# Nystrom attention and two feed-forward layers: scores of both factors in one group of 64x32 products, and k and q of batches 2 and 3 turned by VectorE

## The chip, the core and the metric

One NeuronCore of a Trainium2 chip. The metric is the device time of one execution in microseconds (us); of several runs the median is compared.

## The reference, cut to what matters

Four batches, eight heads, 576 rows, head size 64. Attention is approximated with 32 landmarks per head, the means of 18 rows each, and its output feeds two feed-forward layers.

```
q_lm = q.reshape(B, H, 32, 18, D).mean(axis=3);  k_lm likewise
A  = softmax(q    @ k_lm.T / 8)      # 576 x 32
Bm = softmax(q_lm @ k_lm.T / 8)      # 32 x 32
C  = softmax(q_lm @ k.T    / 8)      # 32 x 576
Z  = six steps of 2 Z - Z @ Bm @ Z   # from a scaled Bm.T
x  = A @ Z @ C @ v                   # to 2304 x 512
h  = x @ w_in;   x = (h * cos(h)) @ w_out          # 512 -> 2048 -> 512
h  = x @ w_in2;  y = prelu(h, alpha) @ w_out2
```

The weights arrive as 64-bit floats and are made into 32-bit ones on the chip.

## The kernel before, in words

**Units.** Attention is computed in eight units, one per batch and group of four heads: `u0`, `u1` (batch 0) and `U2` to `U7` (batches 1 to 3). A unit loads k, q and v, turns k and q so that the head dimension lies on partitions (`kt`, `qt`: two heads hh in the two halves of the partitions, two values bb in the free dimension), forms the landmarks `kq`, and computes two score tables: "c" (k against q's landmarks, tile `sc`) and "a" (q against k's landmarks, tile `sa`). The c table becomes exponentials, is turned and multiplied with v; the a table is turned in 32x32 blocks by VectorE (line 831), made a softmax, turned again and split into two parts for the matmuls of the ticks.

**How batches 2 and 3 turn k and q (`U4` to `U7`).** The load (line 635) is two DMAs of 288 KB for each of k and q, in runs of 256 bytes. TensorE then turns them with 18 transposes of 128x128 per unit (lines 684 and 693), and ScalarE or VectorE copies them out of PSUM: four copies of 512 columns and two of 128. `U2` and `U3` do the same; `u0` and `u1` have their own form. For `U4` to `U7` GpSimd sums the landmarks from `kt` and `qt` (line 727).

**How the scores are formed (`scores`, line 751).** `kq` is kept as block-diagonal pairs of heads: GpSimd sets it to zero once (line 510), and only the halves that belong to a head are written. A product has all 128 partitions as contraction, 64 landmark columns (two heads of 32) and 320 or 256 columns of the sequence. Each table of a unit is four products, two bb times two chunks; the two bb write to different halves of the output's partitions. In `U2` to `U7` the c table is one group of four products and the a table another, each into a pair of "x" banks of PSUM.

**Ticks.** The first feed-forward layer is 128 ticks (`t0` to `t127`). Each has six products h1 (line 1028) into one of two "h" banks, five elementwise steps on ScalarE and VectorE (lines 1033 to 1040; the split of line 397 on GpSimd or VectorE), and four times three products y1 (line 1053) into four "acc" banks. The "h" bank comes free with the product of line 1038 on VectorE. V' (`v_mm`, line 984) prepares each batch's attention for the ticks: eight products of 64 rows by 32 columns by 512, whose row half is bb and whose column group qd is worked out in the loop. After the ticks the second layer runs by a Strassen scheme (lines 1342 to 1423).

**Order.** The string `ORDER` lists every operation as unit:number, with a letter where the engine isn't the first choice (/V VectorE, /A ScalarE, /G GpSimd). Each engine, and SP's queue of DMAs, issues what falls to it in that order and waits in place. `w` operations are fill products on TensorE (line 520).

Of the kernel before, what the change touches and what calls it, by code (L numbers as in the profile page):

```python
# [11 lines left out]
I32 = mybir.dt.int32  # L12
# [8 lines left out]
u0:1 u0:2 u0:4 w:2 w:9 u0:11 w:7 w:6 w:8 w:10 u0:18 u0:7 u0:5 u0:9 u1:1 c2:1 u0:19 u1:2 u0:10/V u0:20 u0:6 u0:21 u0:12  # L21
u0:16 u0:17/V u0:8 u0:24 u0:22 c3:1 u1:4 u1:18 u0:14 u0:13/V c2:2 u0:23 u0:25 u0:26 u0:28 c2:3 c2:4 u0:15/V c3:2 u1:19
u1:20/A u1:21/A w:3 w:1 c3:3 z0:1 u0:27 z0:2 c1:1 z0:3 u0:3 c3:4 u1:5 z0:4 u1:6 w:5 u1:7 u1:8 z0:5 c1:2 z0:6 c1:3 z0:7
z0:8 z0:9 z0:10 z0:11 c1:4 z0:12 u0:31 u1:9 u1:10 u0:29 w:4 u1:22 u1:24 u1:11 u0:37 c0:1 c9:1 u1:23 u1:25 u0:34 z0:13
z0:14 u1:26 u0:30 c0:2 z0:15 u1:16 u1:17 u1:27 u1:28 u0:32 z0:17 z0:16 u1:12 w:11 c0:3 u1:31 u1:14 z0:18 u0:35 u1:13
u1:32 u1:29 c0:4 u1:30 u0:38 u1:34 c9:2 u0:33 u0:39 u1:3 u1:35 c9:3 u1:33 U2:1 u0:36 u1:36 u0:40 z0:19 u1:15 c9:4 u1:37
z0:20 u0:41 w:12 U2:4 u1:38 z0:21 z0:22 u1:39 u1:40 z0:23 z0:24 w:13 c10:1 c11:1 U2:2 u0:42 u0:43 z0:25 w:15 z0:26 w:14
c11:2 u0:44 u0:45 c10:2 w:16 z0:27 z0:28 u1:41 U2:5 U2:6 u1:42 u1:43 z0:29 u1:44 u1:45 c10:3 c4:1 U3:2 U2:13 z0:30 u0:46
U2:14 u0:47 z0:31 c10:4 U2:16/A U2:15/A z0:32 u1:46 z0:33/A z0:34 u0:48 v0:1 v0:2 u1:47 c11:3 v0:3 v0:4 u1:48 v0:5 w:17
U2:10 U2:12/V c4:2 u1:49/V u0:49 U2:11 U2:17 U2:18 U2:19 U2:20 U2:21 U2:22 c11:4 t0:1 t0:2 t1:1 t1:2 c8:1 c4:3 c4:4 U2:7  # L30
t0:3 U2:8 t0:4 c8:2 c8:3 t1:3 U3:1 c8:4 t1:4 c4:5 t0:5 U3:14 U3:13 c5:1 c6:1 U2:9 t0:6 U3:16/A U3:15/A t2:1 c10:5 c7:1
U2:3 t1:5 c5:2 c4:6/V t1:6 t2:2 t3:1 t3:2 c5:3 t2:3 v1:1 v1:2 c5:4 c3:5 t2:4 v1:3 t0:7 t0:8 t0:10 t0:9 t2:5 z1:1 t0:11
t3:3 c5:5 v1:4 v1:5 t2:6 t4:1 U2:27 z1:2 z1:3 t3:4 t1:7 c5:6 U2:28 U2:23 t3:5 t1:10 t5:1 c6:2 t1:11 t4:2 t4:3 U2:25
U2:24 c6:3 c6:4 t3:6 t5:2 U2:30 t5:3 U2:31 c6:5 t2:7 t4:4 t3:7 t5:4 c7:2 t4:5 c7:3 U2:26 t4:6 U2:32 U2:29 t5:5 t6:1 t6:2
U3:4 t4:7 c7:4 c7:5 U3:6 t7:1 U3:5/V c6:6/V t6:3 t7:2 c12:1 c1:5 c13:1 U3:10 t7:3 U3:11 U3:3 c14:1 U3:12 t6:4 U2:33 t1:8
# [297 lines left out]
def kernel(  # L333
# [175 lines left out]
    for p in range(NP):  # L509
        nc.gpsimd.memset(kq[p], 0.0)  # L510
# [100 lines left out]
    def unit(u, tu, ta=None):  # L611
# [147 lines left out]
        for ch in range(2):  # L759
            n = (N0, N1)[ch]  # L760

            def cs(e, ch=ch):
                for x in (ch,) if m == 0 else range(2):
                    for bb in range(2):
                        scores(sc[x], x, 1, kt, bb, p)
# [736 lines left out]
```

## Time and profile before

| | us |
|---|---|
| median of 3 runs (814.96 to 817.45) | 815.19 |
| the profiled execution | 814.85 |
| its span | 813.0 |
| TensorE busy in the span | 799.3 |
| VectorE busy | 594.9 |
| ScalarE busy | 413.0 |
| GpSimd busy | 226.8 |

The profiled execution's own time is 1.85 us above its span. A product in 32-bit floats is two instructions in the trace, so that a group of four is counted as 8 and one of eight as 16; a transpose is one instruction. Matmuls overlap one another in the array: a group's cost on TensorE is read from its start to the start of the next group.

### The profile page before, as it was taken

What the parts mean: (1) busy time and instruction counts of PE and PEld (TensorE: products, weight loads), DVE (VectorE), ACT (ScalarE), POOL (GpSimd) and SP (SyncE); (2) the same over time, 40 slices, a digit from 0 to 9 for tenths busy, and PEclk for the clock granted to TensorE, in tenths of its full rate; (3) what the DMA queues carried; (4) which work ended last, traced back from release to release, by engine and by line L of the source; (5) the groups of instructions that cost most, each with busy time, mean ns of one, the idle gap of its engine ahead of it and who ended that gap; (6) DMA issues with size and microseconds to landing.
All of it is one profiled execution on the core that took longest, in us unless ns stands there. A gap on an engine that the chain in (4) does not pass through costs nothing.

```text
span 813.0 us, 16870 instructions
## 1 busy us (share of the span) xinstructions
PE 799.3 (98%) x6490; PEld 716.1 (88%) x6490; DVE 594.9 (73%) x1234; ACT 413.0 (51%) x930; POOL 226.8 (28%) x250
## 2 busy tenths in 40 slices
PE   9899999999999999999999999999999999999997
PEld 7578899988888999899999888989998989999886
DVE  5899898767977857789779998656656656455653
ACT  5477656767665557667655444422423244323231
POOL 0324413567421022428421114203400232000020
PEclk9999999999999999999999999999999999999999
DMA  8985457749576544744542322301131103120231
GB/s 278 232 235 153 135 160 236 190 106 226 140 261 217 164 142 159 221 150 151 189 135 95 100 79 84 111 27 40 42 89 40 40 27 104 33 71 6 85 107 27
DMA packets 87520, 103.34 MB, mean 127 GB/s; under 512 B 35472, under 2 KB 62608, under 8 KB 87440
## 3 DMA queue, kind: packets, MB, share of 16 engines
q1 hardware_dynamic: 87360, 102.14, 42.8%
q8 instruction: 51, 0.84, 0.4%
q14 instruction: 29, 0.24, 0.1%
q10 hardware_dynamic: 80, 0.13, 0.0%
HBM read 79.96 MB, written 22.28 MB: 126 GB/s over the span
## 4 chain that ended last, share of the span: by engine, by line
PE 68%; DVE 18%; ACT 5%; issue 4%; DMA 3%; POOL 1%; SPq 0%; DVEq 0%; ACTq 0%; POOLq 0%
PE acc L1423 19%; PE acc L1053 15%; PE h L1342 9%; PE h L1028 8%; PE x L1342 7%; DVE m L397 3%; DVE m L1035 1%; DVE m L559 1%; DVE m L1406 1%; DVE m L1038 1%; PE x L751 1%; DVE m L1409 1%; ACT m L1037 1%; DVE m L1365 1%; DMA wi2d<-m 1%
## 5 line engine op out<-in xcount | busy, mean ns | idle before, releaser
L397 POOL TENSOR_TENSOR m<-m,m 128x288 fp32r<-128x288 f32 (+4 forms) x176 | 169.7, 976 | 514.2 <-ACT m L1411 178.9
L1053 PE MATMUL acc<-m,m 128*128 128x288 f32 x1536 | 234.1, 298 | 0.2
L1053 PEld LDWEIGHTS acc<-m,m 128*128 128x128 f32 x1536 | 211.0, 188 | 15.6 <-issue 9.9
L1423 PE MATMUL acc<-m,m 128*128 128x512 f32 x864 | 217.9, 392 | 0.5 <-DVE m L397 0.3
L1423 PEld LDWEIGHTS acc<-m,m 128*128 128x128 f32 x864 | 154.1, 188 | 28.3 <-DVE m L397 1.4
L397 DVE TENSOR_TENSOR m<-m,m 128x512 fp32r<-128x512 f32 (+4 forms) x224 | 139.4, 643 | 43.7 <-ACT m L1411 18.1
L1028 PE MATMUL h<-m,m 128*128 128x288 f32 x768 | 124.6, 299 | 2.4 <-DVE m L1038 2.0
L1028 PEld LDWEIGHTS h<-m,m 128*128 128x128 f32 x768 | 107.8, 188 | 9.4 <-DVE m L1038 6.0
L1342 PE MATMUL h<-m,m 128*128 128x256 f32 x768 | 108.6, 282 | 0.6 <-ACT m L392 0.6
L1342 PEld LDWEIGHTS h<-m,m 128*128 128x128 f32 x768 | 102.6, 189 | 6.7 <-ACT m L392 1.2
L1411 ACT ACTIVATE m<-m 128x512 fp32r<-128x512 f32 (+1 forms) x80 | 46.1, 585 | 91.2 <-DVE m L1409 86.7
L1037 ACT ACTIVATE m<-m,quarter 128x288 f32<-128x288 f32 x128 | 67.4, 534 | 37.7 <-DVE m L1035 36.7
L1342 PE MATMUL x<-m,m 128*128 128x256 f32 x576 | 81.7, 283 | 0.0
L1342 PEld LDWEIGHTS x<-m,m 128*128 128x128 f32 x576 | 76.5, 189 | 3.9 <-DVE m L394 0.3
L1035 DVE SCALAR_TENSOR_TENSOR m<-h,m 128x288 f32<-128x288 f32 x128 | 57.3, 452 | 22.0 <-ACT m L1033 21.4
L1038 DVE TENSOR_TENSOR m<-m,h 128x288 f32<-128x288 f32 x128 | 56.9, 449 | 22.3 <-ACT m L1037 19.6
L392 ACT ACTIVATE m<-h 128x256 f32<-128x256 f32 (+2 forms) x84 | 32.6, 389 | 78.8 <-PE h L1342 64.7
L1040 ACT ACTIVATE m<-m 128x288 fp32r<-128x288 f32 x128 | 55.6, 439 | 33.0 <-DVE m L1038 28.0
L1033 ACT ACTIVATE m<-h 128x288 int32<-128x288 f32 x128 | 51.0, 404 | 32.6 <-PE h L1028 31.4
L1174 ACT ACTIVATE m<-m 128x512 fp32r<-128x512 f32 x68 | 41.5, 625 | 30.1 <-PE h L1342 10.0
L1409 DVE SCALAR_TENSOR_TENSOR m<-m,m 128x512 f32<-128x512 f32 x64 | 45.5, 726 | 0.8
L1365 DVE TENSOR_TENSOR m<-h,m 128x512 f32<-128x512 f32 x32 | 22.0, 687 | 32.8 <-ACT m L392 21.8
(147 smaller groups left out, 771.2 us busy)
## 6 DMA issues: line engine op xcount, KB each, us to landing
m<-in_moe_w_in_dram SPq DMA_DIRECT2D x32, 512.0 KB, 5.0
m<-wi2d SPq DMA_DIRECT2D x56, 256.0 KB, 3.0
m<-in_moe_w_out_dram SPq DMA_DIRECT2D x24, 512.0 KB, 4.5
m<-w1d SPq DMA_DIRECT2D x32, 256.0 KB, 5.6
y1d<-m SPq DMA_DIRECT2D x24, 288.0 KB, 4.0
m<-in_k_dram SPq DMA_DIRECT2D x16, 288.0 KB, 5.2
m<-in_q_dram SPq DMA_DIRECT2D x16, 288.0 KB, 6.0
out_dram<-m SPq DMA_DIRECT2D x35, 128.0 KB, 2.7
```

The costliest lines, as they stand in the source:

```text
L397: ENG[e].tensor_tensor(o, a, b, op=ALU.subtract)
L1028: nc.tensor.matmul(out=hp.t[:, 0:CW], lhsT=w_[:, js], rhs=x[:, cs], start=(i == 0), stop=(i == 5))
L1033: op(act(CW, True), lambda e: nc.scalar.activation(k_.t, hp.t[:, 0:CW], AF.Copy, scale=INV2PI, bias=0.25), r=[hp], w=[k_], target=T + 0.8)
L1035: op(dve(CW), lambda e: nc.vector.scalar_tensor_tensor(u.t, hp.t[:, 0:CW], INV2PI, k_.t, op0=ALU.mult, op1=ALU.subtract), r=[hp, k_], w=[u])
L1037: op(act(CW), lambda e: nc.scalar.activation(u.t, u.t, AF.Sin, scale=2.0 * math.pi, bias=quarter), rw=[u], aset="sin")
L1038: op(dve(CW), lambda e: nc.vector.tensor_tensor(hc.t, u.t, hp.t[:, 0:CW], op=ALU.mult), r=[hp, u], w=[hc], target=T + 2.6)
L1040: op(act(CW), lambda e: nc.scalar.activation(gh.t, hc.t, AF.Copy), r=[hc], w=[gh, gl])
L1053: nc.tensor.matmul(out=yg[o].t[:, 0:CW], lhsT=w_.t[:, sl], rhs=x.t, start=(j == ja and i == 0), stop=(j == jb and i == 2),)
L1342: nc.tensor.matmul(out=rv(k), lhsT=a_.t[:, p, c2, js], rhs=b_.t[:, q_, c2, 0:hw], start=(first and c2 == 0 and i == 0), stop=(c2 == 1 and ...
L1409: op(dve(w), lambda e, m_=m_, hv=hv: nc.vector.scalar_tensor_tensor(m_.t[:, 0:w], hv(), 0.0, m_.t[:, 0:w], op0=ALU.max, op1=ALU.add), r=hr ...
L1411: op(act(w), lambda e, m_=m_, gh=gh: nc.scalar.activation(gh.t[:, 0:w], m_.t[:, 0:w], AF.Copy), r=[m_], w=[gh, gl])
L1423: nc.tensor.matmul(out=ya[n][t].t, lhsT=gv(x_), rhs=r_.t, start=(st and k == 0), stop=(en and k == 2))
```

## The change

1. In every unit a score product is now one head: 64 partitions of contraction, 32 landmark columns, its output in its own column group of 32. In `U2` to `U7` each chunk of the sequence gets one operation with eight such products, four for c and four for a, at eight places of the array (two row halves, four column groups). The c products go to a pair of "x" banks and the a products to a pair of "h" banks. In `u0` and `u1` c and a stay separate, with four products per chunk. `kq` isn't set to zero any more.
2. The a products lie in the column groups that c leaves, so that within each pair of heads their order is exchanged; V' follows with its own qd.
3. In `U4` to `U7` k and q are each loaded by four DMAs in runs of 128 bytes, to 32 partitions each, and VectorE turns each with one 32x32-block transpose of 1152 columns from SBUF to SBUF. The 18 TensorE transposes and six PSUM copies of such a unit are gone. A unit now has 37 operations instead of 44: 4 and 5 are the transposes, 12 and 14 the two groups of scores, 26 and 27 the turns of the a table.
4. `ORDER` is another one from its first line to the first third of the second layer (operations `b2`); the rest is as before.

```
@@
-    for p in range(NP):
-        nc.gpsimd.memset(kq[p], 0.0)
@@
+            elif b > 1:
+                t = sb("raw", [P, RAW], I32)
+
+                def ld(e, t=t, src=src):
+                    for y in range(4):
+                        hh, x = divmod(y, 2)
+                        nc.sync.dma_start(
+                            out=f32(t.t)[32 * y:32 * y + 32, 0:2 * NR * D].rearrange("p (r q i) -> p r q i", r=NR, i=32),
+                            in_=src[b, 4 * c + 2 * hh:4 * c + 2 * hh + 2].rearrange(
+                                "b (q j r) (x i) -> j r (b q) x i", j=32, r=NR, i=32)[:, :, :, x],
+                        )
+                o = loads(4, ld, 4.5, w=[t], after=aft)
@@
+        elif b > 1:
+            for nm, tn in (("kn", "kt"), ("qn", "qt")):
+                T[tn] = atb(1, tn, [P, NR, 2, 64])
+                op(dve(1152), lambda e, t=T[tn], a=nat[nm]: nc.vector.transpose(
+                    out=t.t.rearrange("p r b s -> p (r b s)"), in_=f32(a.t)[:, 0:1152]), r=[nat[nm]], w=[T[tn]])
@@
-        def scores(dst, ch, which, t, bb, pp, swap=0):
+        def scores(ch, *dst):
             n = 64 * (CH[ch][1] - CH[ch][0])
-            nc.tensor.matmul(
-                out=dst.t[64 * (bb ^ swap):64 * (bb ^ swap) + 64, 0:n],
-                lhsT=kq[pp][:, bb, 2 * which:2 * which + 2].rearrange("p h m -> p (h m)"),
-                rhs=t.t[:, CH[ch][0]:CH[ch][1], bb, :],
-            )
+            for bb in range(2):
+                for hh in range(2):
+                    sl = slice(64 * hh, 64 * hh + 64)
+                    for o, which, t in dst:
+                        qd = 2 * bb + hh if which else 2 * (bb ^ c) + (hh ^ 1)
+                        nc.tensor.matmul(
+                            out=o.t[32 * qd:32 * qd + 32, 0:n], lhsT=kq[p][sl, bb, 2 * which + hh],
+                            rhs=t.t[sl, CH[ch][0]:CH[ch][1], bb, :])
 
         sc = pair()
+        sa = (psb("h"), psb("h")) if m else None
@@
+            else:
+                o1 = op(pe(n, 4), lambda e, ch=ch: scores(ch, (sc[ch], 1, kt), (sa[ch], 0, qt)),
+                        r=[kt, qt, *kqb[p]], w=[*(sc[ch:]), sa[ch], at], after=[o1] if ch else [])
@@
-                        qd = 2 * (bb ^ c) + hh
+                        qd = 2 * (bb ^ c) + (hh ^ 1)
```

Of the new order, the lines with the scores of `U4` and of `U6`, in which the two groups are apart and side by side:

```
+V2:3 U4:7 t42:1 t37:9 t42:2 t40:6 t38:11 t38:10 U4:12 t38:9 t38:8 t39:10 t40:7 t42:3 t42:4 t42:5 t42:6 t44:1 U4:26
...
+U5:25 U6:14 U6:12 U6:27 U6:15 U6:13 t46:11 t47:10 e47:6 U6:16 t50:6 U5:30 t51:1 t47:8 t46:9 t47:11 U6:18 U6:17 U7:4
```

## Rows read from the trace of the kernel before

**Rows 1.** The page: busy time by engine, share of the span, instructions

```profile
PE 799.3 (98%) x6490; PEld 716.1 (88%) x6490; DVE 594.9 (73%) x1234; ACT 413.0 (51%) x930; POOL 226.8 (28%) x250
```

**Rows 2.** The page: the chain that ended last, by engine

```profile
PE 68%; DVE 18%; ACT 5%; issue 4%; DMA 3%; POOL 1%; SPq 0%; DVEq 0%; ACTq 0%; POOLq 0%
```

**Rows 3.** Busy us and instructions of each engine by stretch, clock, DMA share

```profile
core 0: us, PE busy (x) PEld busy (x) DVE busy (x) ACT busy (x) POOL busy (x), PEclk, DMA share, GB/s
0.00:20.00 20.00, 18.30 (x236) 15.40 (x236) 10.58 (x34) 10.51 (x19) 1.71 (x10) 1.00 0.89 276
20.00:40.00 20.00, 17.30 (x346) 11.42 (x342) 17.74 (x51) 8.45 (x21) 7.24 (x5) 1.00 0.98 233
40.00:60.00 20.00, 18.46 (x243) 15.00 (x244) 19.20 (x44) 14.63 (x36) 5.70 (x6) 1.00 0.85 237
60.00:80.00 20.00, 20.00 (x240) 16.47 (x239) 19.19 (x54) 15.92 (x34) 8.03 (x7) 1.00 0.61 167
150.00:235.00 85.00, 84.70 (x856) 74.01 (x855) 64.19 (x159) 57.55 (x129) 50.02 (x66) 1.00 0.68 176
```

**Rows 4.** Groups by line and shape: count, busy us and mean ns, PE

```profile
L751 PE MATMUL x<-m,m 128*64 128x320 f32 x48 | 9.1, 457 | 0.3 <-DVE m L991 0.3
L684 PE MATMUL x<-m,m 128*128 128x128 f32 x96 | 12.8, 274 | 0.0
L693 PE MATMUL x<-m,m 128*128 128x128 f32 x12 | 2.4, 281 | 0.9 <-DVE m L991 0.9
```

**Rows 5.** Timeline of PE, 145 to 165 us: start, length, line, count

```profile
147.42 1.03 PE L684 MATMUL x<-m,m 128*128 128x128 f32 x8
148.21 0.64 PE L1053 MATMUL acc<-m,m 128*128 128x288 f32 x3
...
154.16 0.38 PE L693 MATMUL x<-m,m 128*128 128x128 f32 x2
154.29 0.65 PE L1053 MATMUL acc<-m,m 128*128 128x288 f32 x3
...
156.85 1.09 PE L984 MATMUL x<-m,m 64*32 64x512 f32 x16
157.87 1.46 PE L1053 MATMUL acc<-m,m 128*128 128x288 f32 x9
```

**Rows 6.** The chain in order of time: start, us, what

```profile
161.70 1.12 PE x L751 x8
```

**Rows 7.** Groups by line and shape, DVE

```profile
L843 DVE STREAM_TRANSPOSE m<-m 128x576 f32<-128x576 f32 x8 | 6.1, 768 | 0.0
L831 DVE STREAM_TRANSPOSE m<-x 128x320 f32<-128x320 f32 x6 | 3.0, 505 | 1.2 <-PE x L751 1.2
L394 DVE COPY m<-x 128x512 f32<-128x512 f32 x9 | 6.1, 683 | 0.8 <-PE x L684 0.6
L394 DVE COPY m<-x 128x128 f32<-128x128 f32 x3 | 0.8, 288 | 0.3 <-PE x L693 0.3
```

**Rows 8.** Line 635, the loads of k and q of batches 1 to 3

```profile
L635 SPq DMA_DIRECT2D m<-in_k_dram x12: 545/728/2616, 20.0 to 191.3; - x12
L635 SPq DMA_DIRECT2D m<-in_q_dram x12: 541/702/2130, 24.7 to 194.8; - x12
DMA to landing us min/median/max: 4.0/5.5/8.4
```

**Rows 9.** What PE waited for: us in total, times, longest us

```profile
PE h L1028 <- DVE m L1038: 2.0, 5, 1.1
```

**Rows 10.** Groups by line and shape, POOL: the clearing of `kq`

```profile
L510 POOL MEMSET m<- 128x256 f32 x4 | 1.1, 311 | 0.0
```

More of the change, by code (lines that the diff above doesn't have):

```diff
@@ L26 @@
[L26 to L35, printed above, removed]
@@ L226 @@
[L226 to L230 removed]
+u0:1 u0:4 w:8 w:9 w:5 w:2 w:10 w:4 w:1 u0:7 u1:1 u0:9 u0:5 u1:4 u0:6/V w:7 u0:18 u0:10/V u0:2 u0:19 c0:1 u0:11 u0:12
@@ new lines @@
+t91:8 t91:9 t94:6 t92:10 t92:11 t92:8 t93:8 t93:10 t97:1 t94:7 s56:3 V2:18 t95:4 t95:5 t95:6 t93:11 t92:9 t96:1 t93:9
+t97:2 t97:3 t97:4 c47:2 t95:7 t97:5 c47:3 t94:9 t98:1 t94:10 t94:11 t94:8 t95:8 t96:2 t96:3 t96:4 t96:5 s56:11/V t97:6
+V1:22 t98:2 t96:6 c47:4 t96:7 t99:1 s56:12 t99:2 s56:1 t98:3 V1:23 t98:4 V2:15 c51:1 c48:5 t95:11 t95:10 t95:9 c46:5
+c49:1 V2:19 t97:7 t99:3 e95:4/V t98:5 e95:2 t100:1 t99:4 e95:5 e95:1 c47:5 e95:6 V3:17 V3:16 V3:15 V3:18 t98:6 c51:2
+t99:5 t98:7/V c51:3 t96:11 s56:5 t97:11 t100:2 t96:10 c49:2 s56:14 t101:1 t96:8 t97:8 t96:9 t97:10 e95:3 V2:22 s56:9
@@ new lines @@
+t102:10 t104:4 V3:21 t104:5 y0:25/V y0:2 y0:7 t104:6 t104:7/V t107:2 c51:4 t107:3 t106:1 t105:7/V t106:2 t107:4 y0:15
+y0:16 y0:3 V3:23 y0:26/V t106:3 t107:5 c50:1 t106:4 t106:5 y0:4/V t103:11 t103:10 t104:11 t103:8 y0:6 t106:6 t107:6
+y0:37 t106:7/V y0:35 t104:9 t104:8 t105:8 t108:1 t109:1 t105:9 t108:2 t108:3 t109:2 t109:3 t107:7/V y0:5 t108:4 c51:5
+t108:5 y0:19 t104:10 t105:10 t105:11 t106:11 t107:11 t110:1 c50:2 y0:8/V c52:3 c50:3 y0:13 y0:27 y0:17 t109:4 y0:33
+t110:2 t110:3 t109:5 t106:10 t107:10 t106:8 t106:9 y0:11 t110:4 t108:6 c50:4 t111:1 t107:9 t108:7/V t108:10 t108:9
@@ new lines @@
+c55:3 t121:5 t119:10 t119:11 t118:9 t122:1 t119:9 t120:11 t120:10 o1:3/V t121:6 t121:7/V o2:2 o2:3 o9:3/V o10:1 s57:3
+o8:1 s57:4 o11:1 t123:1 o4:5 t122:2 t122:3 t122:4 o10:2 t122:5 t121:11 t123:2 o8:2 t123:3 t123:4 t123:5 t122:6 t122:7/V
+o10:3/V t120:9 t121:10 t120:8 t121:8 t124:1 t125:1 t121:9 t123:6 t122:9 t123:7/V t123:9 o11:2 t124:2 t122:10 t122:8
+t125:2 t124:3 t122:11 t123:11 t123:8 s57:5 o11:3/V t125:3 t124:4 t125:4 o8:3 t124:5 t124:6 o4:1 t125:5 t126:1 t125:6
+t124:7/V t126:2 o12:5 o4:2 o4:3 o4:4 o4:6 t126:3 t125:7/V o4:7 o4:8 t127:1 t127:2 o12:1 c54:5 t126:4 t127:3 t126:5
@@ new lines @@
+t126:9 t127:11 s57:21 e127:5 e127:6 t127:9 b2:4 b0:25 e127:2 e127:1 o13:1 s58:1 o13:5 e127:3 b0:19 b2:5 b1:22 s57:22/V
+s57:16/V b1:15 s58:2 b0:20 b0:21 b2:6 b0:27 b2:3 b2:7 b0:28 b0:18 o13:2 o13:3 b1:16 b2:9 b2:8 b2:10 b3:1 b3:2 o13:4
+b0:29 b1:23 b1:17 b1:21 b2:11 o13:6 o13:7 o13:8 o6:1 b2:12 b2:13 s58:5 b1:24 s58:3 s58:9 s58:7 b1:25 b3:4 s58:4 b3:3
+b0:26 b3:5 s58:6 b3:6 b2:22 b2:14 b2:15 s58:8/V s58:11/V b3:7 o6:2 b2:23 b1:18 b2:16 b1:19 b1:27 b1:20 b1:26 b1:29 o6:3
+b3:8 s58:12 s58:10/V b3:9 s58:14/V o13:9 o13:10/V o6:5 b2:17 o6:4 b2:24 b2:25 o14:1 s58:13/V s58:17/V s58:15 s58:18
@@ new lines @@
+b3:10 b4:1 b2:18 s58:20/V s58:19/V s58:21 b3:11 b4:2 b1:28 s59:1 s58:22 b3:12 b3:13 s58:16/V s59:2 b4:4 b4:5 b2:21 b4:3
+s59:3 b3:22 b3:14 o14:2 s59:4 b3:15 b4:6 b4:7 b3:23 b4:8 b3:16 b2:20 b4:9 b3:24 b3:17 s59:7 b2:26 b4:10 b3:25 o14:3
+s59:8/V b4:11 s59:11 b4:13 b4:12 b2:19 b2:28 b3:18 s59:12 b4:14 b4:22 o6:6 b4:15 o14:4 s59:14/V b4:23 b3:20 o6:7
+s59:13/V b2:29 b3:28 b3:21 b2:27 b5:1 b4:16 o6:8 b4:17 b5:2 b4:24 o6:9 s59:5 b5:4 o6:10/V b3:26 b5:5 s59:6/V b4:25 o14:5
+b5:3 s59:9 s59:15 o7:1 b4:18 b5:7 s59:17 b5:6 s59:10/V b5:8 s59:18 s59:16/V s59:20/V s59:19/V s59:21 s59:22/V o14:6
@@ new lines @@
+b9:10 b9:11 s61:4 s61:5/V b8:25 b9:13 b9:12 b7:37 s62:2 b8:18 b10:1 b10:2 b8:20 b9:14 b10:4 b10:3 b9:15 b9:22 b10:5
+b9:23 b10:6 b9:16 b8:19 b8:26 b10:7 b9:24 b10:8 b9:17/G b10:9 b10:10 b10:13 b10:11/V b10:12 b9:25 b8:27 b9:18 b11:1
+b8:28 b11:2 b10:14 b10:22 b10:15 b11:4 b9:26 b9:20 b8:21 b11:3 s61:8 s61:6 b10:16 s62:4 s61:7/V b10:23 b11:5 b11:7 b7:31
+s62:3 b11:8 b11:6 b9:28 b8:29 b10:24 b11:9 b9:21 b10:17 s62:5/V b11:10 b9:29 b11:13 b11:11/V b10:25 s61:9/V b11:12
+b10:20 b11:14 b10:21 b11:22 b11:23 b11:15 b10:28 b10:18 b9:19 b12:1 b10:29 b11:16 b9:27 b11:17 b10:26 b11:21 b10:19
@@ new lines @@
+b12:2 b12:3/V b12:4 b12:5 b12:7 b12:6 b11:24 b12:8/V b12:9 b12:10 b13:1 b12:11 b12:13 b13:2 b10:27 b12:12 b11:25/G
+b11:20 b13:4 b13:3/V b12:14 b12:15 b12:22 b13:5 b11:29 b13:7 b12:23 s62:6 b13:6 b13:8 s62:8 b12:16 s62:7 b12:24 y2:1
+b13:9 b11:18 b12:25/G y2:3/V s62:9/V y2:2 b13:10 b13:11 b12:17 y2:21 b11:26 b12:21 b11:19 y2:22 b13:12 b13:13 b13:14
+y2:4 y2:23 b13:22 y2:24 b11:28 b13:23 b13:15 b13:16 b11:27 b12:29 b14:1 b13:17 b13:24 b12:20 b13:25 b12:18 b14:2 b14:3/V
+y2:25/V b12:26 b13:21 b14:4 b14:5 b13:18 b14:7 b14:6/V b14:8/V y2:26/V y2:5/V b14:9 b14:10 b15:1 b12:28 b13:29 y2:29
@@ new lines @@
+b15:18 b15:35 b17:1 b16:11 b16:12 b16:13 b16:14 b15:32 b15:26 b16:15 b15:36 b16:22 b15:33/V b16:23 b15:27 b17:2 b14:19
+s63:8 b17:3 b16:16 b17:4 b16:17 b17:5 b17:6/V s63:6 s63:9/V b17:7 s64:4 s63:7/V b17:8/V b17:9 b16:18 b15:37 b16:20
+b17:10 b18:1 b17:11 b17:13 s64:5/V b18:2 b17:12 s64:2 b15:34 s64:3 b18:4 b17:14 b18:3 s65:1 b17:15 b18:5 s65:2 b18:7
+b18:6 b18:8 b18:9 b18:10 b19:1 b19:2 b14:27 s64:8 s64:6 b19:4 b16:24 b16:25 s64:7/V b15:19 s65:3 b19:5 b17:16 s65:4
+b15:29 b16:28 b16:26 b15:30 b17:22 s65:5/V b17:23 b17:17 b16:21 b18:13 b19:3 b18:11 b17:24 b18:12 b16:19 b16:29 b18:14
@@ new lines @@
+b17:25 b16:27 b19:7 b17:18 b18:15 b17:21 b18:16 b18:17 b18:22 b18:23 b18:24 b19:6 b19:8 b18:25 b17:26 b17:29 b17:20
+b18:18 b17:28 b19:9 b18:26 b19:10 s64:9/V b19:13 b19:11/V b19:12 b18:20 b19:14 b19:22 b17:19 b19:15 b19:16 b18:28 b20:1
+b17:27 b19:17 b19:23 b18:21 b19:24 b18:19 b20:2 b18:29 b20:4 b20:3 b20:5 b18:27 b20:7 b19:21 b19:18 b20:6/V b20:8/V
+b19:25 b20:9 b20:10 b20:11/V b20:13 b20:12 b19:29 b20:22 b20:14 b19:19 b19:20 b21:1 b20:15 b19:28 b19:26 b21:2 b20:23
+b20:16 s65:8 s65:6 b20:24 b20:17/G b21:3/V b21:4 b21:5 b20:20 b21:6 s65:7/V b20:25/G s65:9/V y3:1 b15:28 y3:2 b21:7
@@ L231 @@
+b36:13 b38:1 b36:14 b37:7 b38:2 b37:12 b38:3 b38:9 b38:4 b38:5 b39:1 b37:13 b38:6/G b39:3 b38:10 b39:4 b37:8 b39:2 b39:5
+b38:11 b38:7 b38:12 b37:14 b39:6 b39:9 b38:13 b39:10 b38:8 b39:11 b39:12 b39:7 b38:14 b39:13 b39:8 b39:14 b39:16 b39:17
+b39:15 b39:19 b39:18
 """
@@ L760, in unit @@
             n = (N0, N1)[ch]
[L762 to L765, printed above, removed]
-            if m == 0 or ch == 0:
-                o1 = op(pe(n if m == 0 else S, 4), cs, r=[kt, kqb[p][1]], w=[sc[ch]] if ch else sc, after=[o1] if ch else [])
+            if m == 0:
+                o1 = op(pe(n, 4), lambda e, ch=ch: scores(ch, (sc[ch], 1, kt)), r=[kt, kqb[p][1]],
+                        w=[sc[ch]] if ch else sc, after=[o1] if ch else [])
+            else:
+                o1 = op(pe(n, 4), lambda e, ch=ch: scores(ch, (sc[ch], 1, kt), (sa[ch], 0, qt)),
+                        r=[kt, qt, *kqb[p]], w=[*(sc[ch:]), sa[ch], at], after=[o1] if ch else [])
             op(dve(n), lambda e, ch=ch, n=n: nc.vector.reduce_max(mx.t[:, ch:ch + 1], sc[ch].t[:, 0:n], axis=AX.X),
@@ L816, in unit @@
            r=[pc, rs], w=[o_], target=tu)
-        sa = pair()
-        at = atb(m, "at", [P, NBK, M])
+        sa = sa or pair()
         mxa, sma = atb(m, "amx", [P, NBK, 1]), atb(m, "asm", [P, NBK, 1])
@@ L826, in asc @@
                 for x in range(2):
-                    for bb in range(2):
-                        scores(sa[x], x, 0, qt, bb, p, c)
-            if ch == 0:
+                    scores(x, (sa[x], 0, qt))
+            if m == 0 and ch == 0:
                 op(pe(S, 4), asc, r=[qt, kqb[p][0]], w=[*sa, at])
```

361 lines of the change are left out of this document (160 added, 201 removed).

## The prediction

> **What bounds the kernel now.** I first read the busy line of the page: TensorE is busy 98% of the span, VectorE 73% [rows 1]. A busy TensorE need not be the bound, since its matmuls overlap, so I read the chain next: 68% of it is TensorE's own work, 18% VectorE's [rows 2]. Then busy time by stretch, because a share of the whole says nothing of a stage [rows 3]. Three stages differ. Up to 60 us TensorE is not full: it lacks 1.7, 2.7 and 1.5 us in three stretches of 20, while VectorE has 17.7 and 19.2 in the last two and the DMA share is 0.85 to 0.98. There VectorE and the loads set the pace. From 60 us TensorE has 20.00 of 20, although VectorE has 19.19. From 150 to 235 us, where the units of batches 2 and 3 mostly lie beside the ticks, TensorE has 84.70 of 85 and VectorE 64.19, or 76%. So in the stage that the change mostly touches, what is taken from TensorE is taken from the time, as long as the other engines keep up. The clock is granted at 1.00 in all these stretches, so no term is needed for it.
>
> **The change part by part.**
>
> *Transposes gone from TensorE.* The trace has 96 transposes of the groups of eight and 12 of the pairs, over six units [rows 4]; four of the six lose theirs. From start to start of what follows, a group of eight takes 148.21 - 147.42 = 0.79 us and a pair 154.29 - 154.16 = 0.13 [rows 5]. A unit has two groups of eight and one pair: 1.71 us. Four units: 6.8 us, all of it TensorE's own stream between ticks.
>
> *Scores.* A group of four products (8 instructions) takes 1.12 us on the chain [rows 6], and there are 12 such groups in `U2` to `U7` (the 48 instructions of 320 columns in [rows 4] are four to a group): 13.4 us. What eight 64x32 products at once take, V' shows: it has two row halves and four column groups, each of its two banks gets products from both row halves, and its 16 instructions of 512 columns take 157.87 - 156.85 = 1.02 us [rows 5]. For 576 columns that is 1.02 x 576/512 = 1.15. Five units have their two groups side by side on TensorE; in `U4` four operations lie between them, for which I add 0.2: 6 x 1.15 + 0.2 = 7.1 us. Gain 13.4 - 7.1 = 6.3. The bounds are 6.7 (twelve groups become six of 1.12) and nothing (the eight take turns by halves).
> The Trainium skill, TensorEngine Tiling (Array Packing), under Restrictions and Gotchas, says that different row tiles cannot access one PSUM bank simultaneously. The new groups do just that, and by that rule each group would take twice as long and the 6.3 would be nothing. This trace disagrees with it for products in different column groups, by the 1.02 us above.
>
> *VectorE's turns.* Eight transposes of 1152 columns come in. The trace has none of that size. From 320 to 576 columns the price goes from 505 to 768 ns [rows 7], 1.03 ns a column; 576 columns more make 0.77 + 0.59 = 1.36 us each, 10.9 us in all. Of the copies that go away, the old order gave VectorE seven of 512 columns and two of 128: 7 x 0.683 + 2 x 0.288 = 5.4 us [rows 7]; the other 15 leave ScalarE, which is not short. VectorE's balance is +5.5 us. In the stretch 150 to 235 us that makes (64.2 + 5.5) of about 85 - 11 us, or 94%. Nothing of it is on the path as long as TensorE has products queued; the cover is the same one that 60 to 80 us shows (VectorE 96%, TensorE 20.00). The dear end is 40 to 60 us, with VectorE at 96% too and 1.5 us in 20 lost [rows 3]: over some 75 us that would be 5.8. I take 1 us, near the first, since ticks run in full in both.
>
> *Loads in 128-byte runs.* Four DMAs instead of two per tensor, 16 more in all. Issuing one takes about 0.7 us of SP's queue at the median (up to 2.6) [rows 8], so each tensor holds SP 1.4 us longer, and the stores of `y1d` and reloads for V' that are behind it move by as much. The landing takes 5.5 us at the median. A DMA has as many runs as before (1152) and half the bytes; I therefore take the same 5.5, one issue pair later: 1.4 us. The cheap end is no delay, the dear one a doubling, 5.5 us. VectorE waits in place in front of each turn, with the ticks' steps of lines 1035 and 1038 behind it, and TensorE behind those. The order puts loads ahead of the turns, and two "h" banks and the y1 products of earlier ticks let TensorE go on for about a tick. I count 0.5 us in all, with 0 as the low end.
> Another page of the Trainium skill, DMA: Bandwidth & Descriptors, under Why small descriptors are slow, gives each packet about three cycles besides one for every 32 bytes. By that estimate 128-byte runs would hold the DMA engines 2 x 7/11 = 1.27 times as long as 256-byte ones; no row here prices a 128-byte run.
>
> *"h" banks.* The a table now takes both "h" banks, and h1 of the next tick waits until VectorE has turned it: 0.505 us for the first bank [rows 7], after the group has ended. Now TensorE loses 2.0 us in all on VectorE's last read of "h" [rows 9]. Six units with y1 products in between: I take 0 to 0.4 us each, 0.5 in all.
>
> *At nothing.* The clearing of `kq`, 1.1 us of GpSimd in the first microseconds [rows 10], while TensorE is still in its fill products. The scores of `u0` and `u1`: per chunk four products side by side instead of two, as long as one. V' with exchanged column groups: the same eight places.
>
> *The new early order.* Up to 60 us TensorE lacks 1.7 + 2.7 + 1.5 = 5.9 us [rows 3]; a new order could win at most that and lose about as much. VectorE has the same operations to do for `u0` to `U3` as before. I take 0, with 3 either way.
>
> Sum: -6.8 - 6.3 + 1 + 0.5 + 0.5 = -11.1 us. Against the profiled execution's 814.85 (span 813.0 and 1.85 around it) that is 803.7; the median of the runs is 0.34 above that execution, so 804.0 against 815.19.
>
> **The rivals.**
>
> *Row halves take turns in a bank.* The products of the two halves run one after the other, a group of eight takes 2 x 1.15 us, and the scores gain nothing: 804.0 + 6.3 = 810.3. (This is what the rule of the Trainium skill's TensorEngine Tiling (Array Packing) would give.) For it: the a and c products of one chunk share two banks between both halves. Against it: V' does the same at full pace [rows 5]. 7%.
>
> *VectorE becomes the bound.* Turns of 1.36 us stand in VectorE's queue ahead of the ticks' steps, both "h" banks are held until it comes to them, and the early stretches are at 96% already. At the rate of 40 to 60 us the loss is 5.8 instead of 1, and the h banks cost 0.5 us more per unit, 3: 804 + 7.8 = 811.8; half of it, 808. For it: the 94%. Against it: 60 to 80 us. 17%.
>
> *Loads late, slower than before.* If the four DMAs of a tensor land one after another, a turn is 5.5 us late; what TensorE has queued covers one tick's y1, 12 products or about 1.6 us, and some 3.5 us are left per tensor, eight times 28: 804 + 28 = 832; with half of the tensors 818. It decides from 11.1/8 = 1.4 us of TensorE's idling per tensor. For it: DMA share 0.68 in that stretch, an issue that took 2.6 us at worst. Against it: a DMA's landing here goes with its runs, not its bytes. 8%.
>
> *It comes out even*, as losses of the early order and of VectorE add up to the gain: 813 to 817. 5%.
>
> **How the numbers follow.** The forecast, 800 to 807, has the remaining 63%. About 0.3%, 2.4 us, is what a measurement of this kernel can tell from no change. Faster: forecast, the first rival and nearly all of the second, 0.86. Within: 0.05, slower: 0.09. The range goes down to 799 (all 13.1 and 3 of the early order, 815.2 - 16.1 = 799.1), and up to 812, which takes in the halves' rival and VectorE's 811.8.
>
> **What would show it.** Transposes of lines 684 and 693 down to 32 and 4 instructions. Score groups of 16 instructions, both chunks within 1.2 us from start to start; 2 us and more would show the halves taking turns. VectorE's transposes of 1152 columns near 1.36 us. TensorE waiting for VectorE's line 831 under 0.4 us per unit. The stretch from tick 40 to 64 with VectorE at 90 to 95% and TensorE still full. The prediction is wrong if VectorE waits for `in_k_dram` or `in_q_dram` by microseconds, or if TensorE's gaps ahead of line 1028 sum to over 5 us.

## The result, and the profile after

The changed kernel takes 804.39 us in the median of 4 runs (802.92 to 807.22), against 815.95 for the kernel before on the same chip: ratio 0.9861, interval 0.9826 to 0.9896. The forecast was 804.0 in a range of 799 to 812. Below, "after" is the profiled execution of that run (805.5 us), and "again" that of a second one (803.25 us).

The busy line and the chain of the page after, which answer to [rows 1, 2]:

```profile
PE 786.5 (98%) x6546; PEld 705.3 (88%) x6546; DVE 589.9 (73%) x1228; ACT 406.8 (51%) x927; POOL 214.2 (27%) x237
```

```profile
PE 78%; DVE 10%; DMA 5%; ACT 3%; issue 2%; SPq 1%; POOL 0%; ACTq 0%; DVEq 0%
```

TensorE's busy time falls by 12.8 us, and its own work has 78% of the chain instead of 68. Busy time by stretch of the kernel after (us and instructions by engine, clock, DMA share), and under it the stretch 145 to 230 us of the kernel before:

```profile
core 0: us, PE busy (x) PEld busy (x) DVE busy (x) ACT busy (x) POOL busy (x), PEclk, DMA share, GB/s
20.00:40.00 20.00, 18.29 (x364) 11.94 (x364) 17.91 (x57) 8.22 (x23) 4.89 (x4) 0.91 1.04 251
40.00:60.00 20.00, 17.94 (x227) 13.65 (x218) 19.31 (x45) 17.17 (x38) 8.73 (x7) 1.00 0.92 254
...
145.00:230.00 85.00, 83.95 (x998) 73.74 (x1001) 74.28 (x172) 61.76 (x138) 50.83 (x66) 1.00 0.86 201
```

```profile
145.00:230.00 85.00, 84.70 (x833) 74.23 (x832) 66.44 (x163) 60.81 (x136) 49.35 (x64) 1.00 0.67 172
```

In the stage of the late units VectorE goes from 66.4 to 74.3 of 85 us, the DMA share from 0.67 to 0.86, and TensorE is hardly less full. To see where the time went, I count six products of h1 (line 1028 before, 1045 after) to a tick, and note when a tick's first one starts (us):

```
                 tick 0   tick 16   tick 32   tick 64   last tick   end of span
before            41.23     95.44    138.70    253.72     416.21       813.0
after             41.95     97.19    138.16    242.95     405.10       803.7
again             40.82     96.07    136.96    241.73     403.62       801.4
```

Nearly all of the gain arises between ticks 32 and 64, where the units of batches 2 and 3 lie: 115.0 us become 104.8 in both. The first 16 ticks lose 1.0 us, and the next 16 gain 2.3. These starts don't enclose the same work, as a count of TensorE's instructions between them shows. Ticks 0 to 16 hold 147 y1 instructions instead of 135, and ticks 16 to 32 hold 192 instead of 207: at 0.133 us each, 1.6 and 2.0 us that the new order only moved. From tick 32 to 64 the 72 transposes are gone (6.8 us by the prices of [rows 5]), seven score groups of the old form (7.9) have become four units' groups of the new one (5.8), 12 y1 instructions are gone (1.6), and one V' has come in (1.0): 9.5 of the 10.2 us. From the last tick to the end "again" takes 397.8 us, against 396.8 before, with three y1 instructions more.

**TensorE.** Its groups by line and shape after (count, busy us and mean ns):

```profile
L770 PE MATMUL x<-m,m 64*32 64x320 f32 x48 | 4.9, 441 | 0.3 <-DVE m L834 0.2
L698 PE MATMUL x<-m,m 128*128 128x128 f32 x32 | 4.1, 272 | 0.0
L770 PE MATMUL h<-m,m 64*32 64x256 f32 x48 | 4.0, 385 | 0.0
L707 PE MATMUL x<-m,m 128*128 128x128 f32 x4 | 0.8, 286 | 0.8 <-DVE m L1008 0.8
```

The transposes are down to 32 and 4, as forecast [rows 4]. The timeline of TensorE after has `U4`'s two score groups apart (of each group's 16 instructions the first, and what follows the group):

```profile
166.03 0.45 PE L770 MATMUL x<-m,m 64*32 64x320 f32 x1
...
166.79 1.46 PE L1070 MATMUL acc<-m,m 128*128 128x288 f32 x9
...
169.37 0.40 PE L770 MATMUL x<-m,m 64*32 64x256 f32 x1
...
169.97 2.27 PE L1070 MATMUL acc<-m,m 128*128 128x288 f32 x15
```

Eight products take 0.76 us for 320 columns and 0.60 for 256: the first instructions of all eight start within 0.1 us (166.03 to 166.13), so they run together, though both row halves write to both banks. So the rule of the Trainium skill's TensorEngine Tiling (Array Packing), Restrictions and Gotchas, doesn't slow products in different column groups here, as [rows 5] had it. But other units don't reach these times. `U5`, where the second chunk follows at once:

```profile
181.77 0.45 PE L770 MATMUL x<-m,m 64*32 64x320 f32 x1
...
182.33 0.59 PE L770 MATMUL x<-m,m 64*32 64x256 f32 x2
182.93 0.40 PE L770 MATMUL h<-m,m 64*32 64x256 f32 x1
...
183.52 0.66 PE L1070 MATMUL acc<-m,m 128*128 128x288 f32 x3
```

```profile
182.42 0.45 DVE L1055 TENSOR_TENSOR m<-m,h 128x288 f32<-128x288 f32 x1 [0.41 <-ACT m L1054]
```

The second chunk's first c product starts at 182.33, its first a product at 182.93: the second h bank is still held by the tick before, until VectorE's line 1055 ends (the last line, from VectorE's timeline, at 182.87). The group takes 1.75 us.

**VectorE's turns and the loads** (groups of VectorE; then the loads of k and q of batches 2 and 3 on SP, and their time to landing):

```profile
L688 DVE STREAM_TRANSPOSE m<-m 128x1152 f32<-128x1152 f32 x8 | 10.9, 1368 | 0.0
```

```profile
L633 SPq DMA_DIRECT2D m<-in_q_dram x16: 585/848/2562, 140.5 to 194.9; - x16
L633 SPq DMA_DIRECT2D m<-in_k_dram x16: 584/850/2006, 148.1 to 181.8; - x16
...
DMA to landing us min/median/max: 3.1/4.6/6.8
```

A turn takes 1.368 us (forecast 1.36), with no idle time in front of any. A DMA lands after 4.6 us at the median (4.3 in "again"). The 5.5 of [rows 8] has the loads of batch 1 in it; those of batches 2 and 3 alone took 5.3 before. An issue takes 0.85 us.

**What TensorE waited for after** (us in total, times, longest):

```profile
PE h L680 <- DVE m L909: 2.0, 1, 2.0
...
PE h L1045 <- DVE m L1055: 1.3, 2, 1.0
...
PE h L1045 <- DVE m L848: 0.6, 1, 0.6
```

Waiting for VectorE's turn of the a table (line 848) costs 0.6 us once. The longest wait is new and lies early. VectorE's timeline after shows why:

```profile
18.31 0.22 DVE L902 TENSOR_REDUCE m<-h 128x2 f32<-128x64 f32 x1
20.50 0.43 DVE L552 TENSOR_SCALAR m<-m 128x512 int32<-128x512 int32 x1 [1.96 <-DMA m<-in_moe_w_in_dram]
20.84 0.22 DVE L909 TENSOR_TENSOR m<-h,m 128x64 f32<-128x64 f32 x1
```

In the new order a conversion (line 552), whose weights have not landed, stands ahead of the step that frees an h bank, and TensorE waits behind it. In the same execution the clock then falls to its lower level (1.2 GHz, shown as 0.50 of full speed), here by stretches of 2 us:

```profile
20.00:22.00 2.00, 0.80 (x4) 0.60 (x4) 1.50 (x5) 0.76 (x3) 0.00 (x0) 0.77 0.93 222
22.00:24.00 2.00, 2.00 (x18) 0.63 (x17) 1.96 (x10) 1.88 (x7) 0.00 (x0) 0.50 1.01 227
24.00:26.00 2.00, 2.00 (x28) 1.47 (x27) 1.45 (x9) 1.02 (x4) 0.00 (x0) 0.88 1.25 224
```

### The profile page after: what moved, and what is told of

The parts are those of the page before. It is cut to its first block, busy times and chain, and to the rows that moved or that the text cites. A ratio compares the mean times of both kernels' runs of the same rounds, so it can differ in the third digit from the quotient of the medians.

```text
span 803.7 us, 16970 instructions
## 1 busy us (share of the span) xinstructions
PE 786.5 (98%) x6546; PEld 705.3 (88%) x6546; DVE 589.9 (73%) x1228; ACT 406.8 (51%) x927; POOL 214.2 (27%) x237
## 4 chain that ended last, share of the span: by engine, by line
PE 78%; DVE 10%; DMA 5%; ACT 3%; issue 2%; SPq 1%; POOL 0%; ACTq 0%; DVEq 0%
PE acc L1440 23%; PE acc L1070 19%; PE h L1359 11%; PE h L1045 9%; PE x L1359 8%; DMA m<-in_moe_w_in_dram 3%; DVE m L396 2%; PE h L1404 1%; PE x L1404 1%; PE x L1001 1%; PE x L938 1%; DVE m L1055 1%; DVE m L556 1%; DVE m L554 1%; DVE m L1052 1%
## 5 line engine op out<-in xcount | busy, mean ns | idle before, releaser
L396 POOL TENSOR_TENSOR m<-m,m 128x288 fp32r<-128x288 f32 (+4 forms) x172 | 164.6, 971 | 519.6 <-ACT m L1428 179.0
L1070 PEld LDWEIGHTS acc<-m,m 128*128 128x128 f32 x1536 | 211.0, 188 | 16.3 <-issue 11.1
L1359 PE MATMUL x<-m,m 128*128 128x256 f32 x576 | 81.8, 283 | 0.0
L391 ACT ACTIVATE m<-h 128x256 f32<-128x256 f32 (+3 forms) x86 | 33.3, 391 | 76.9 <-PE h L1359 64.4
```

The costliest lines, as they stand in the source:

```text
L396: ENG[e].tensor_tensor(o, a, b, op=ALU.subtract)
L1070: nc.tensor.matmul(out=yg[o].t[:, 0:CW], lhsT=w_.t[:, sl], rhs=x.t, start=(j == ja and i == 0), stop=(j == jb and i == 2),)
L1359: nc.tensor.matmul(out=rv(k), lhsT=a_.t[:, p, c2, js], rhs=b_.t[:, q_, c2, 0:hw], start=(first and c2 == 0 and i == 0), stop=(c2 == 1 and ...
```

## The experiments

All are edits of the changed kernel. "Stretch" is the time from tick 32's to tick 64's first product in the profiled execution: 104.8 us with the change, 115.0 before. The kernel before, measured beside each set of runs, took 815.31 us beside the first four, 816.02 beside the next four and 816.94 beside the last, so medians of different sets are to be compared by their ratios too.

**The changed kernel again.**

> The changed kernel once more, as the base for the runs beside it. Theory: about 803 to 805 us, ratio to the kernel before 0.985 to 0.988; some executions have a stretch near 22 us at half the granted clock, and those are 2 to 4 us longer than those without. Rival: the spread of its executions has nothing to do with that stretch, and the long ones show the clock at 1.00.

Measured: 803.77 us (803.25 to 806.66), ratio 0.9869 (0.9846 to 0.9893). The profiled execution has the same early wait (2.2 us for line 909) and a clock of 1.00 throughout. In both executions the early wait ends at 21.20 us. By 26 us the one whose clock fell is 1.1 us behind (a score group at 22 us takes 2.08 us in it and 1.11 in the other), and it stays 1.1 to 1.2 behind up to tick 64. So the drop costs about 1.1 us when it occurs, less than expected. A late start of the ticks alone doesn't prove a drop: in the run with half turns below, whose clock stays at 1.00, tick 0 starts at 42.2, after two waits for VectorE's line 955 (1.0 us together). An execution of 803.37 has a mean clock of 0.997 and one of 803.25 has 1.000: most of the spread comes from elsewhere.

**The conversion behind the small steps.**

```diff
-z0:1 u0:3 z0:2 c9:2 u0:28 z0:3 z0:4 u0:27 c9:3 u1:24 u1:22 u1:3 u1:12 u1:16 u1:17 u1:13 U2:1 c10:1 z0:5 u0:31 u0:37
+z0:1 u0:3 z0:2 u0:28 z0:3 z0:4 u0:27 u1:24 u1:22 u1:3 u1:12 u1:16 u1:17 u1:13 U2:1 c10:1 z0:5 c9:2 c9:3 u0:31 u0:37
```

> Two operations of one weight conversion (c9:2, c9:3) stand behind three small steps of batch 0 in the order instead of ahead of them, so that VectorE frees the h bank before it waits for the weights' load. Theory (the order around 20 us lets TensorE stand still for 2.0 us and the clock then drops): TensorE's wait for line 909 is gone, the clock stays at 1.00 up to 60 us, and the median is 1.5 to 3 us below that of the changed kernel, near 802. Rival (VectorE's chain sets the pace up to 60 us, and TensorE's standing still there is free): within 0.7 us of it.

Measured: 804.68 us (804.14 to 805.58), ratio 0.9871 (0.9850 to 0.9892). That is 0.9 us above the changed kernel beside it, just outside the rival's 0.7 and within the spread; the ratios are the same (0.9871 and 0.9869). The theory falls. The wait for line 909 is gone, and another takes its place (what TensorE waited for in this kernel):

```profile
PE h L802 <- ACT m L794: 1.7, 1, 1.7
```

The clock fell in this execution too, and tick 0 starts at 42.0. That fits the rival: the waits show the other engines' chain, and moving one doesn't shorten it.

**The old score products in the new place.**

```diff
+    for p in range(NP):
+        nc.gpsimd.memset(kq[p], 0.0)
...
-                        nc.tensor.matmul(
-                            out=o.t[32 * qd:32 * qd + 32, 0:n], lhsT=kq[p][sl, bb, 2 * which + hh],
-                            rhs=t.t[sl, CH[ch][0]:CH[ch][1], bb, :])
+                        out=o.t[x:x + 64, 0:n],
+                        lhsT=kq[p][:, bb, 2 * which:2 * which + 2].rearrange("p h m -> p (h m)"),
+                        rhs=t.t[:, CH[ch][0]:CH[ch][1], bb, :])
```

> The score products alone are as they were (128 partitions by 64 columns from block-diagonal landmarks, cleared once), in the new operations, banks and order. Theory (eight small products run together): 5.5 to 7 us longer than the changed kernel, near 811, and a chunk's group takes 1.1 to 1.3 us instead of 0.6 to 0.75. Rival (the small products took turns, and the gain comes from the transposes and the order): within 1 us.

Measured: 808.52 us (806.41 to 811.18), ratio 0.9919 (0.9898 to 0.9941): 4.75 us above the changed kernel run beside it, clear of the rival and below the theory. The timeline of TensorE in this kernel, `U4`'s groups:

```profile
168.12 0.76 PE L770 MATMUL x<-m,m 128*64 128x320 f32 x4
168.71 0.71 PE L770 MATMUL h<-m,m 128*64 128x320 f32 x4
169.34 1.46 PE L1071 MATMUL acc<-m,m 128*128 128x288 f32 x9
...
171.53 0.65 PE L770 MATMUL x<-m,m 128*64 128x256 f32 x4
172.01 0.60 PE L770 MATMUL h<-m,m 128*64 128x256 f32 x4
172.55 0.67 PE L1071 MATMUL acc<-m,m 128*128 128x288 f32 x3
```

1.22 and 1.02 us, against 0.76 and 0.60. Over `U2` to `U7` the groups sum to 13.0 us from start to start, against 9.2 in the changed kernel ("again"; by unit 1.82, 1.60, 1.34, 1.76, 1.54 and 1.13): 3.8 less. `U5`'s group is 2.09 here with no gap inside, which fits the c products covering the wait for the h bank; the small ones are done before it ends. The 4.75 us are not all in these groups, though. The stretch is 106.6 us, 1.8 more, and the first 16 ticks, with `U2` and `U3`, take 0.6 more: 2.4 for 3.8 us of longer groups, so TensorE makes up a part. Against "after", whose clock fell as here, this execution's span is 4.6 us longer. The rest of that lies before tick 0 (0.9, where the edit also undoes the scores of `u0` and `u1` and clears `kq`), between ticks 16 and 32 (0.6, cause not found) and behind tick 64 (0.7, within what executions differ by there).

**The transposes back on TensorE.**

```diff
+                    if b > 1:
+                        for r in range(NR):
+                            nc.tensor.transpose(
+                                sc[ch].t[:, 0:P], (kt, qt)[ch].t[:, r].rearrange("p b s -> p (b s)"), ident)
                     scores(ch, (sc[ch], 1, kt), (sa[ch], 0, qt))
```

> In each of the four units of batches 2 and 3, 18 transposes of 128 columns are done on TensorE beside the turns on VectorE, ahead of the score products, into the same bank (overwritten after). Theory (TensorE's stream sets the time there): 6.8 to 8 us longer than the changed kernel, near 812. Rival (VectorE or the loads set the pace in that stage now, so that TensorE has slack): under 4 us.

Measured: 811.18 us (808.67 to 812.64), ratio 0.9942 (0.9920 to 0.9964), 7.4 above the changed kernel; the stretch is 111.9 us, 7.1 more. TensorE's stream sets the time there, as the theory has it. Undone one at a time, scores and transposes cost 12.2 us together, more than the 11.56 gained, so the new order need not explain any of it; a run with both undone at once was not made.

**The old loads.**

```diff
-                    for y in range(4):
-                        hh, x = divmod(y, 2)
+                    for hh in range(2):
                         nc.sync.dma_start(
...
+                            in_=src[b, 4 * c + 2 * hh:4 * c + 2 * hh + 2].rearrange("b (p r) d -> (b p) r d", r=NR),
```

> k and q of batches 2 and 3 are loaded as before, in two DMAs of 256-byte runs each, and the new turns run over that layout; so the scores of these two batches are computed from other values. Theory (the 128-byte loads are hidden): within 1 us of the changed kernel, and the DMA share from 145 to 230 us falls from 0.86 toward 0.7. Rival (the loads or their issues hold VectorE's turns back): 2 us or more shorter, near 801.

Measured: 803.53 us (801.19 to 804.13), ratio 0.9833 (0.9814 to 0.9852). The median is 0.24 below the changed kernel's in the run before; against the kernels before on each side the ratio is 0.36% lower, 2.9 us, with intervals that overlap. The trace decides it: the stretch is 104.9 us, no shorter, although the DMA share falls to 0.73 (busy time by stretch in this kernel, and the landing of its loads of batches 2 and 3):

```profile
145.00:230.00 85.00, 83.96 (x982) 73.76 (x980) 74.27 (x171) 61.34 (x137) 50.53 (x67) 1.00 0.73 198
...
DMA to landing us min/median/max: 3.5/4.6/6.9
```

The old loads land after 4.6 us too. From the last tick to the end this execution takes 395.1 us, against 397.8 in "again", with the same order there; but the ten profiled executions of the changed kernel and its versions take anything from 395.1 to 399.0 there. So in their own stage the 128-byte loads are hidden.

**Half turns, and turns done twice.**

```diff
-                    out=t.t.rearrange("p r b s -> p (r b s)"), in_=f32(a.t)[:, 0:1152]), r=[nat[nm]], w=[T[tn]])
+                    out=t.t.rearrange("p r b s -> p (r b s)")[:, 0:576], in_=f32(a.t)[:, 0:576]), r=[nat[nm]], w=[T[tn]])
```

```diff
-                op(dve(1152), lambda e, t=T[tn], a=nat[nm]: nc.vector.transpose(
-                    out=t.t.rearrange("p r b s -> p (r b s)"), in_=f32(a.t)[:, 0:1152]), r=[nat[nm]], w=[T[tn]])
+                op(dve(1152), lambda e, t=T[tn], a=nat[nm]: [nc.vector.transpose(
+                    out=t.t.rearrange("p r b s -> p (r b s)"), in_=f32(a.t)[:, 0:1152]) for _ in range(2)],
+                   r=[nat[nm]], w=[T[tn]])
```

> VectorE turns only half of k and q in batches 2 and 3 (576 of 1152 columns), and the other half of the turned tiles keeps older values. Theory (the turns lie beside TensorE's work, and cost about 1 us): 0.5 to 1.5 us shorter than the changed kernel. Rival (VectorE is the bound from 145 to 230 us): 3 to 5 us shorter, the 5.5 us of VectorE's time that it saves.

> VectorE does each turn of batches 2 and 3 twice, 10.9 us more. Theory (VectorE has 74 of 85 us in that stretch, so about all of the added time still fits, but TensorE's waits grow): 2 to 5 us longer than the changed kernel. Rival one (VectorE is the bound already): 9 to 11 us longer. Rival two (VectorE has slack everywhere): under 1 us.

Measured: half turns 803.55 us (801.86 to 805.13), ratio 0.9843 (0.9823 to 0.9862), the stretch 103.9, 0.9 shorter. Turns done twice 813.99 us (812.23 to 815.87), ratio 0.9972 (0.9961 to 0.9984), 10.2 above the changed kernel (8.4 by the ratios); the stretch is 114.7, 9.9 more. Busy time by stretch in the two, in that order:

```profile
145.00:230.00 85.00, 84.46 (x1015) 74.40 (x1013) 71.31 (x173) 62.35 (x138) 51.05 (x67) 1.00 0.84 205
```

```profile
145.00:230.00 85.00, 77.18 (x773) 67.01 (x772) 75.22 (x156) 54.06 (x125) 47.77 (x63) 0.98 0.75 173
```

This is the misjudged one. For the theory of the turns the first run holds: half of a turn takes 0.77 us, so that VectorE is spared 4.8 us, and that is worth 0.9. But the second run lies where its first rival had it: 11.1 us more of VectorE's work lengthen the stretch by 9.9, although VectorE is busy no more than 75.2 of 85 us there. What TensorE waited for in it, from 138 to 256 us:

```profile
PE h L1046 <- DVE m L1056: 5.1, 6, 1.8
PE acc L1071 <- DVE m L1091: 2.0, 1, 2.0
```

From tick 32 to 64 all of TensorE's waits sum to 8.0 us, against 1.25 in "after". The five over 0.6 us, 6.6 in all, each begin between 0.6 us before and 0.9 us after the end of a pair of turns, which holds VectorE for 2.75 us in one piece, with the ticks' steps behind it. The clock falls here as well (0.58 from 182 to 186 us), right behind the wait of 2.0 us; at the 1.1 us of the early drop that is some further 1 us, by estimate. So I had read the 11 us in which VectorE stood idle as free, and they did not take this work up. Whether the whole of VectorE's load or the length of one block does it was not tested: in this run the second turn always follows the first at once. The waits right behind the pairs speak for the block.

**y1 products between the chunks, alone and with half turns.**

```diff
-... U3:17 U3:19 z1:15 U3:18 t3:11 t3:9 ...
+... U3:17 t3:11 U3:19 z1:15 U3:18 t3:9 ...
...
-... U5:13 U5:14 U6:9 U5:15 U5:16 t44:11 U5:27 t47:1 ...
+... U5:13 t44:11 U5:14 U6:9 U5:15 U5:16 U5:27 t47:1 ...
...
-... U6:14 U6:12 U6:27 U6:15 U6:13 t46:11 t47:10 ...
+... U6:14 t46:11 U6:12 U6:27 U6:15 U6:13 t47:10 ...
```

> In three units one group of y1 products is moved between the two chunks of the scores in the order, where now the second chunk waits for an h bank that the tick before holds (0.4 to 0.6 us of standing still inside the group). Theory: these gaps are gone, and the median falls by 0.8 to 1.4 us, to about 802.7. Rival (VectorE's chain passes there, so that the wait moves on): within 0.4 us of the changed kernel.

> The y1 groups between the chunks of the scores, as before, and the half turns of VectorE (k and q of batches 2 and 3 turned for 576 of 1152 columns). Moving the y1 groups closed the gaps inside the score groups and the same time went elsewhere. Theory (VectorE's chain in that stretch took the gain back): with VectorE relieved, the stretch from tick 40 to tick 64 is 1 us or more shorter than with the half turns alone (where it is 82.2 us). Rival (the gaps were covered, that is TensorE catches up by itself): 82.2 us again, within 0.4.

Measured: alone 804.98 us (803.36 to 805.62), ratio 0.9857 (0.9840 to 0.9874); with half turns 804.13 us (801.13 to 806.56), ratio 0.9853 (0.9830 to 0.9877). Alone that is 1.2 us above the changed kernel by the medians and 1.0 below it by the ratios, so the trace has to decide. Without the y1 products between them the score groups get shorter in `U5` (1.76 to 1.29) and `U6` (1.54 to 1.28) and hardly in `U3` (1.60 to 1.55), but the stretch stays at 104.7 alone and 103.8 with half turns. Behind `U5` the time comes back as a wait in the unit's next step (timeline of TensorE, the first of the two):

```profile
186.60 0.66 PE L802 MATMUL x<-m,m 128*128 128x128 f32 x4 [0.28 <-ACT m L794]
```

Both of my theories fall: the gaps were covered, and VectorE's turns aren't what took the gain back. The number 82.2 in the second expectation was misread; from tick 40 to 64 the trace of the half turns has 81.9 us, and this run has 81.8.

No version tried beats the changed kernel by more than its spread. The spread itself has a place. In all three executions without an edit in it the stretch takes 104.8 us; tick 0 starts anywhere from 40.0 to 42.3 us (42.8 with the old score products), and from tick 64 to the end, where all have the same order, the ten executions take 558.2 to 561.5 us. That is why I judge a stage by its stretch.

## Why the prediction was right, point by point

- **The total.** 11.1 us of gain were forecast, and 11.56 measured (815.95 to 804.39; the interval of the ratio makes 8.5 to 14.2).
- **Transposes, 6.8 us.** Put back, they cost 7.4 (7.1 in the stretch). Right.
- **Scores, 6.3 us.** This step was mis-sized. That eight products run together was right (0.76 and 0.60 us where a group stands free). But the groups' sum fell from 13.6 (12 groups at 1.12 or 1.19) to 9.2, that is by 4.4, not 6.3. Undoing them cost 4.75 in the median, of which the trace has 2.4 in the stretches where these groups lie. The sum took side-by-side chunks for the good case and `U4`'s split for the one that costs 0.2 more. It is the other way round: `U4` has 1.34 us, while four of the five with their chunks side by side have 1.54 to 1.82, because inside the group a chunk waits: in `U2`, `U3` and `U5` for line 1055 and the "h" bank that it reads, in `U6` for line 834, which reads an "x" bank, and in `U2`'s second chunk for ScalarE's line 730. Only `U7`, with 1.13, has the forecast's 1.15. The sign given for it, 1.2 us for both chunks, thus failed in five of six units.
- **"h" banks, 0.5 us.** Waiting for the turned a table costs 0.6 us, as forecast. Of the other end of the same resource, banks that the ticks still hold when the scores want them, the term said nothing; those are the gaps inside the groups. That they cost nothing once more when closed (the two runs with y1 between) speaks for TensorE making them up behind.
- **VectorE's turns, 1 us.** 1.368 us each; halving them wins 0.9 us in the stretch. The size was right, but the balance of +5.5 us was not: VectorE's busy time fell by 5.0 us over the whole execution, among others because all nine copies of 512 columns went, not seven, and the new order gave other small steps to ScalarE. It rose by 7.9 us in the stage of the late units. From tick 40 to 64 VectorE is busy for 72.5 of 82.8 us, or 88%, a little under the 90 to 95% given as a sign. The cover was thinner than I made it: of turns twice as long next to nothing was covered.
- **Loads, 0.5 us.** No wait of VectorE for `in_k_dram` or `in_q_dram`, and no gain in the stretch with the old loads. The rival that had them late fell: in the changed kernel a DMA of 1152 runs of 128 bytes lands as soon as one of 256 (4.6 us each). That landing goes with the runs and not the bytes was no more than an assumption when the prediction used it against this rival; these two medians bear it out.
- **The early order, 0 with 3 either way.** Up to tick 16 the new order is behind by 0.6 us ("again") or 1.75 (with the drop of the clock), with a net 0.6 us more of y1 and V' done by then. Within the bounds.
- **After the ticks.** Nothing was set for it. "again" takes 1.0 us longer there than the kernel before, "after" 1.8, but the 396.8 of before lies inside the 395.1 to 399.0 of the ten executions, so no loss is shown. In "again" two waits there are longer than before (1.15 us for ScalarE's line 391, 0.71 for VectorE's line 1055).

Put together from what was measured, 7.1 for the transposes and 4.4 for the scores, less 0.9 for the turns and 0.6 for the a table, make 10.0 us. The mechanism of the prediction stands: TensorE's stream sets the time in the stage of the late units, and what was taken from it came off the time. That the total came within 0.5 us is luck in part: the scores' term was 1.9 too large, and executions of one kernel differ by some 4 us. What stays open is the cause of that spread, before tick 0, where the clock's drop explains about 1.1 us of it, and behind tick 64.

## What to carry to other kernels

Small products at different places of the array pay by their number only while their output banks are free; count for each bank who holds it when the products are due, not only who waits for it afterwards. An engine's idle time in a stage isn't room for any work: price a move onto it by doubling it as well as by halving it, and look at what waits behind one block. A wait that is removed by moving one entry of an order is worth measuring at a later point of the same execution, since here it came back each time. And before a gain is read from the starts of ticks, count what was done between them.

## What the runs showed of the hardware that I had not expected

Halving the run from 256 to 128 bytes, with the number of runs per DMA kept (1152), left the landing at 4.6 us at the median, although a DMA moves half the bytes, and raised the DMA share of the stage from 0.73 to 0.86 (old and new loads in the changed kernel). The Trainium skill's DMA: Bandwidth & Descriptors, Why small descriptors are slow, has small packets cost more per byte; the share agrees in its direction, and the time did not depend on it here. In the packets of the two traces one of 128 bytes holds its DMA engine for 13 ns at the median and one of 256 bytes for 18, so the same bytes take 1.44 times as long, more than the prediction's estimate of 1.27. The clock fell in one execution after TensorE had stood still for 2.0 us, and stayed at 1.00 in another after 2.2 us at the same place.
